# A new issue order for the same instructions: dynamic convolution, LayerNorm and a two-layer FFN on one core

## The chip, the cores and the metric

One NeuronCore of one Trainium2 chip. The metric is device time in microseconds (us), the median of several executions of the whole program.

## What is computed

The inputs are `x` (8 x 4224 x 192, float32), `weight_gen` (8 x 4224 x 8 x 7), a LayerNorm gain and two float64 weight matrices (192 x 768 and 768 x 192). The reference, cut to what matters:

```
w = softmax(weight_gen, axis=-1)                      # 8 heads, 7 taps
y[b,s,h] = sum_k w[b,s,h,k] * x_padded[b, s+k, h]     # causal, 24 channels a head
xn = (y - mean) / sqrt(var + 1e-6) * g_ln
out = y + max(xn @ w_ch1, 0) @ w_ch2
```

## The kernel before

The 33792 tokens lie as 264 columns of 128 partitions. Columns are worked in parts (`PARTS`), parts in chunks of 4 or 6 columns, and the FFN in 66 groups of 4 columns (`NT`).

**Convolution.** For each chunk VectorE (DVE) makes seven products, as three pair instructions and one single one (`mul`, L511). GpSimd (POOL) sums them: two accumulating DMAs (L517, steps `d0`, `d1`) add one half of a pair to the other in memory, and four tensor additions (L514, steps `a0` to `a3`) collect the rest. For the first three chunks (`DIRECT`) TensorE (PE) sums the products with matmuls against an identity (L532, `z0` to `z3`). The softmax weights come in 23 blocks (`SOFT`), spread over DVE, POOL and ScalarE (ACT).

**Norm and transposition.** ACT takes sums and squares of y (L564, L569), scales (`xh`, L615) and rounds to float16 (`hi`, L635); POOL makes the rounding rest (`lo`, L648); a transposing DMA from the SP queue (`turn`, L652) writes `xT`.

**FFN.** A group is three units (`unit`, L670, 36 pairs of matmuls of 64 rows each) and two output halves (`p0`, `p1`, L721, 72 pairs of 64 rows). A unit fills one of two PSUM buffers `ph`. ACT reads it (`relu`, L685, into `hh`), then DVE (`hlo`, L687), and only then can the next unit with that buffer start. PE runs two units of group g, `p0` of group g-1, the third unit, `p1` of g-1. Between the halves an empty SP instruction (`hop`, L731) passes a semaphore on. DVE adds the output to y (`f`, L773) and SP stores it (`u`, L781). The last group's output is made by `output` (L750).

**Weights.** They are brought from float64 to pairs of float16 at the start: `from_double` (L833 to L849), `w_scale` (L860 to L876, with a PE sum, a root on ACT and a reciprocal on DVE), then for the first layer L902 on ACT, the subtraction L905 on POOL and four copies L909 on SP that swap the halves of `c_w`; for the second layer L935 and L936 on ACT and L938 on POOL (all three have the key `w_s2`). `wake` (L642) is 11 matmuls whose result is not used.

**Order.** Nothing is scheduled by the framework (`manual_schedule`). Every step is recorded by `op` with a number from the table `PLACE` (key, then one number for each use), and `Plan.order` issues the steps in the order of these numbers. The numbers also pick buffers: a step that first uses a buffer takes the one whose last user stands earliest. And an accumulating DMA and a transposing one never run together: each waits for the last one of the other kind that stands ahead of it (`o.behind`):

```
for o in plan.order():
    made[o] = o.fn()
    if o.behind:
        tc.add_manual_dep(made[o].ins, made[o.behind].ins.name, apart, reason="transfers kept apart")
```

Of the kernel before, what the change touches and what calls it, by code (L numbers as in the profile page):

```python
# [31 lines left out]
    'wload': (3, 9, 33, 42, 82, 86, 121, 257, 191, 373, 568, 527, 770, 1053, 851, 1068, 1156, 1216, 1427, 1301,  # L32
        1465, 1705, 1809),
    'load': (26, 12, 32, 37, 85, 87, 102, 103, 84, 120, 298, 261, 337, 260, 421, 466, 456, 526, 338, 569, 642,
        641, 756, 712, 769, 783, 849, 885, 978, 1067, 979, 1162, 1159, 1163, 1302, 1343, 1368, 1369, 1572, 1426,
        1566, 1569, 1613, 1806, 1768, 1769, 1808, 1938, 1905, 2076, 2134, 2035),
    'w_load': (40, 11, 13, 0, 1, 2),
    'w_load2': (58,),
    'w_as': (67,),
    'w_av': (41, 44, 65, 73),  # L40
    'w_an': (80,),
    'w_cs': (20,),
    'w_cv': (15, 17, 22, 23),
    'w_cn': (45,),
    'w_s1': (81, 88, 97, 104, 112),
    'w_h': (122, 123, 125, 127),
    'w_l': (153, 156),
    'w_m': (190, 193, 195, 192),
    'w_c2s': (71, 124, 146),
    'w_c2v': (72, 74, 76, 78, 91, 105, 130, 135, 137, 139, 161, 163),  # L50
    'w_c2n': (93, 144, 168),
    'w_s2': (169, 171, 182, 184, 212, 206, 207, 213),
    'max': (4, 10, 34, 43, 89, 136, 138, 352, 234, 446, 665, 608, 868, 1070, 935, 1103, 1258, 1261, 1474, 1430,
        1592, 1712, 1837),
    'sub': (5, 18, 51, 110, 111, 203, 320, 431, 551, 653, 750, 844, 967, 1148, 1090, 1243, 1406, 1441, 1581,
        1684, 1812, 1850, 1947),
    'exp': (6, 19, 52, 115, 114, 227, 321, 436, 552, 659, 751, 860, 983, 1166, 1114, 1255, 1418, 1459, 1582,
        1700, 1825, 1875, 1964),
    'sum': (7, 21, 66, 131, 133, 242, 350, 495, 553, 664, 752, 929, 1009, 1168, 1126, 1260, 1431, 1480, 1591,
        1719, 1834, 1907, 1991),  # L60
    'rcp': (8, 25, 70, 141, 175, 293, 384, 505, 573, 689, 802, 930, 1011, 1170, 1197, 1289, 1501, 1500, 1628,
        1720, 1880, 1960, 2043),
    'inv': (14, 29, 77, 162, 221, 324, 471, 545, 655, 746, 879, 947, 1078, 1202, 1259, 1388, 1536, 1540, 1644,
        1754, 1928, 2006, 2044),
    'mul': (16, 31, 90, 185, 315, 416, 525, 639, 742, 831, 933, 1018, 1128, 1231, 1328, 1433, 1537, 1636, 1738,
        1823, 1930, 2039, 2131),
    'keep': (24, 54),
# [16 lines left out]
    'copy': (53, 94, 126),  # L84
    'sums': (55, 57, 96, 99, 142, 140, 176, 177, 244, 246, 247, 255, 291, 295, 332, 326, 367, 396, 401, 397,
# [7 lines left out]
    'squares': (56, 68, 98, 100, 148, 147, 178, 180, 245, 251, 252, 256, 296, 306, 334, 333, 386, 398, 409, 412,  # L93
# [7 lines left out]
    'rstd': (69, 101, 149, 181, 253, 281, 335, 413, 492, 560, 627, 710, 801, 904, 1001, 1113, 1213, 1298, 1386,  # L101
        1502, 1601, 1702, 1819, 1900, 2005, 2100, 2199, 2285, 2325),
    'newton': (75, 108, 165, 186, 274, 286, 353, 414, 496, 577, 635, 721, 806, 916, 1012, 1116, 1220, 1307,
# [13 lines left out]
    'wake': (208,),  # L117
# [885 lines left out]
```

## Time and profile before

| what | value |
|---|---|
| runs | 869.25 us median (866.22, 869.25, 870.33) |
| profiled execution | span 867.2 us, mean granted TensorE clock 0.987; the page gives no other time for it |
| busy: PE, DVE, ACT, POOL | 95%, 89%, 79%, 78% of the span |
| instructions | 37431 |

The span runs from the first to the last instruction of one execution, and lies inside the spread of the three runs. Times in the rows below are us from the start of that span unless a column says ns. "PEld" is the weight load that runs beside a matmul; "SPq" is a DMA's issue on the SP queue. [...]

### The profile page before, as it was taken

The numbers are of one execution on the slowest core, as the hardware profiler recorded it, in microseconds if no ns is written. First come the engines' busy times: TensorE is split into PE (matmuls) and PEld (weight loads), VectorE is DVE, ScalarE is ACT, GpSimd is POOL, SyncE is SP. The second block draws the span as 40 slices with busy tenths as digits, with TensorE's granted clock in tenths as the row PEclk, the third lists the DMA queues.
The fourth block names the chain that finished last, engine by engine and source line by source line (L and its number), as shares of the span: only waits on it lengthen the run. The fifth ranks groups of instructions, "written<-read, shape, count | busy, mean of one in ns | idle before, by whom it ended". The sixth has DMA issues, their size and how long they took to land.

```text
span 867.2 us, 37431 instructions
## 1 busy us (share of the span) xinstructions
PE 823.4 (95%) x16665; PEld 787.7 (91%) x16665; DVE 772.1 (89%) x796; ACT 683.7 (79%) x1781; POOL 679.6 (78%) x390
## 2 busy tenths in 40 slices
PE   3857999999999999999999999999999999999997
PEld 2526999999999999999999999999989999999997
DVE  6899999999999999999999999999989989874442
ACT  2798898799678889889888789787887888796631
POOL 3399999899889999897887889888976788885100
PEclk9968999999999999999999999999999999999999
DMA  7768868988897958988899698878948569565123
GB/s 193 190 127 166 166 163 184 200 176 180 194 193 151 220 94 188 213 181 180 160 205 195 149 213 175 165 139 187 207 99 200 120 151 190 124 127 106 40 76 110
DMA packets 137465, 140.89 MB, mean 162 GB/s; under 512 B 107479, under 2 KB 109015, under 8 KB 137303
## 3 DMA queue, kind: packets, MB, share of 16 engines
q1 hardware_dynamic: 123175, 88.95, 44.9%
q0 software_dynamic: 13824, 49.55, 29.6%
q8 instruction: 130, 2.13, 1.1%
q14 instruction: 32, 0.26, 0.1%
q10 hardware_dynamic: 304, 0.00, 0.0%
HBM read 36.43 MB, written 25.95 MB: 72 GB/s over the span
## 4 chain that ended last, share of the span: by engine, by line
PE 68%; DVE 9%; issue 2%; DVEq 0%
PE ph L670 34%; PE po L721 34%; DVE pr L511 4%; DVE hlo L687 2%; DVE y L511 1%; DVE y L773 1%; PE ph L750 1%; DVE sm L449 0%; DVE mx L440 0%; DVE wn L465 0%; DVE wn L460 0%; DVE wn L461 0%; DVE wn L459 0%; DVE wn L599 0%; DVE wn L601 0%
## 5 line engine op out<-in xcount | busy, mean ns | idle before, releaser
L514 POOL TENSOR_TENSOR y<-y,pr 128x1152 f32<-128x1152 f32 (+1 forms) x192 | 474.5, 2499 | 39.0 <-DVE pr L511 22.1
L670 PE MATMUL ph<-xT,c_w 64*128 64x256 f16 x7128 | 420.0, 270 | 10.5 <-DVE hlo L687 7.8
L670 PEld LDWEIGHTS <-c_w 64*128 64x128 f16 x7128 | 377.6, 94 | 28.3 <-issue 13.5
L721 PE MATMUL po<-c_w2h,hh 64*128 64x192 f16 x3120 | 392.5, 243 | 1.4 <-issue 1.0
L721 PE MATMUL po<-c_w2h,hlo 64*128 64x192 f16 x3120 | 392.4, 243 | 0.5 <-issue 0.5
L721 PE MATMUL po<-c_w2l,hh 64*128 64x192 f16 x3120 | 392.4, 243 | 0.0
L721 PEld LDWEIGHTS <-hh 64*128 64x128 f16 x6240 | 345.7, 94 | 2.8 <-issue 1.9
L511 DVE TENSOR_TENSOR pr<-x,wn 128x2304 f32<-128x2304 f32 (+1 forms) x150 | 332.5, 2226 | 6.6 <-POOL y L514 1.8
L687 DVE SCALAR_TENSOR_TENSOR hlo<-ph,hh 128x1024 f16<-128x1024 f32 x198 | 239.2, 1219 | 57.2 <-ACT hh L685 56.9
L685 ACT ACTIVATE hh<-ph 128x1024 f16<-128x1024 f32 x198 | 200.3, 1015 | 105.2 <-PE ph L670 101.7
L721 PEld LDWEIGHTS <-hlo 64*128 64x128 f16 x3120 | 225.5, 94 | 0.7 <-issue 0.7
L648 POOL TENSOR_TENSOR hl<-xh,hl 128x768 f16<-128x768 f32 x66 | 115.0, 1748 | 44.5 <-ACT hl L635 33.0
L615 ACT ACTIVATE xh<-y,s 128x192 f32<-128x192 f32 x264 | 125.5, 535 | 16.1 <-DVE s L603 12.5
L569 ACT ACTIVATE junk<-y,s 128x192 f32<-128x192 f32 x264 | 119.6, 453 | 6.9
L517 POOL DMA_DIRECT2D pr<-pr x96 | 94.4, 1082 | 37.3 <-DMA xT<-hl 14.2
L564 ACT ACTIVATE junk<-y 128x192 f32<-128x192 f32 x264 | 95.1, 360 | 13.6 <-POOL y L514 7.2
L773 DVE SCALAR_TENSOR_TENSOR y<-po,c_fs,y 128x768 f32<-128x768 f32 (+1 forms) x80 | 67.9, 860 | 5.4 <-PE po L721 5.4
L511 DVE TENSOR_TENSOR y<-x,wn 128x1152 f32<-128x1152 f32 (+1 forms) x51 | 60.0, 1181 | 0.1
L635 ACT ACTIVATE hl<-xh 128x768 f16<-128x768 f32 x66 | 55.0, 837 | 2.1 <-DMA xT<-hl 1.1
L564 ACT ACTIVATION_READ_ACCUMULATOR junk<-y 128x1 f32 x264 | 49.5, 188 | 0.0
L569 ACT ACTIVATION_READ_ACCUMULATOR junk<-y,s 128x1 f32 x264 | 49.4, 187 | 0.0
L532 PE MATMUL ph<-pr,ident 128*128 128x384 f32 x72 | 27.1, 531 | 16.5 <-DVE pr L511 15.6
(76 smaller groups left out, 298.5 us busy)
## 6 DMA issues: line engine op xcount, KB each, us to landing
pr<-pr POOLq DMA_DIRECT2D x60, 576.0 KB, 7.8
x<-in_x_dram SPq DMA_DIRECT2D x30, 576.0 KB, 6.3
out_dram<-y SPq DMA_DIRECT2D x30, 576.0 KB, 5.2
pr<-pr POOLq DMA_DIRECT2D x36, 384.0 KB, 5.8
x<-in_x_dram SPq DMA_DIRECT2D x20, 384.0 KB, 5.5
out_dram<-y SPq DMA_DIRECT2D x20, 384.0 KB, 5.3
w<-in_weight_gen_dram SPq DMA_DIRECT2D x21, 336.0 KB, 5.8
pr<-in_moe_w_ch_dram SPq DMA_DIRECT2D x1, 1152.0 KB
```

What stands on the lines that cost most here:

```text
L511: E.tensor_tensor(out=ov, in0=xv, in1=wv, op=ALU.mult)
L514: Q.tensor_tensor(out=flat(0), in0=flat(0), in1=flat(k), op=ALU.add)
L517: return Q.dma_start(flat(to), flat(k), accum_op=ALU.add, max_dma_last_dim=CHUNK * D * 4)
L564: A.activation(junk, at(y)[:, j, :], AF.Identity, scale=-1.0 / D, accum_out=at(s4)[:, 3, t : t + 1])
L569: A.activation(junk, at(y)[:, j, :], AF.Square, bias=at(s4)[:, 3, t : t + 1], accum_out=at(s4)[:, 0, t : t + 1])
L615: A.activation(paired(xh, t), at(y)[:, i, :].rearrange("p (c q) -> p c q", q=P // 2), AF.Identity, bias=at(s4)[:, 3, g + t : g + t + 1], s ...
L648: lambda xh=xh, hl=hl: Q.tensor_tensor(out=halves(hl, True), in0=pairs(xh), in1=halves(hl, False), op=ALU.subtract),
L670: T_.matmul(ph[:, r, v * 2 * P : (v + 1) * 2 * P], W["w1"][rows, WB[r][c], w, f : f + P], xv[rows, a, c, :, :], start=(v == 0 and k == 0), ...
L685: lambda: A.activation(at(hh)[:, us, :], at(ph), AF.Relu), [ph], [(hh, u)])
L687: lambda: V.scalar_tensor_tensor(out=at(hlo)[:, us, :], in0=at(ph), scalar=0.0, in1=at(hh)[:, us, :], op0=ALU.max, op1=ALU.subtract),
L721: made.append(T_.matmul(at(po)[:, z, e * D : (e + 1) * D], token(b, 2 * z + e, j)[rows], W[w][rows, j, :], start=(ph == 0 and e == 0 and k ...
L773: V.scalar_tensor_tensor(out=ysl, in0=at(po)[:, zs[0] : zs[-1] + 1, : 2 * D], scalar=W["fs"][:, 0:1], in1=ysl, op0=ALU.mult, op1=ALU.add)
```

## The change

Only the numbers of `PLACE` differ. No step is added or removed, no buffer pool, size or instruction changes; which buffer of a pool a step gets does follow from the new numbers. The table is four lines longer, so every line number behind it grows by 4 (L670 is L674, and so on). PE's order is the same but for one exchange; of DVE's 626 steps 451 stand elsewhere, of ACT's 770 621, of POOL's 383 271, of SP's 266 196, by at most 33 places. The table's rows tell nothing by themselves; the two lines on PE's exchange and the copies of `c_w`:

```diff
-    'wake': (208,),
+    'wake': (159,),
-    'w_s2': (169, 171, 182, 184, 212, 206, 207, 213),
+    'w_s2': (178, 202, 203, 207, 230, 220, 226, 231),
-    'w_m': (190, 193, 195, 192),
+    'w_m': (141, 139, 148, 186),
...
```

On PE, `wake` (11 pairs of L642) now stands ahead of the sum L860 of the second layer's weights; before it stood behind it.

The SP queue just ahead of the first unit (`c_w` is the first layer's weights, `xT` the transposed input, `w` softmax input, `x` the convolution's input). Before:

```order
L909 DMA c_w1_127<-c_w1_127 64x1536
L422 DMA w1_65<-in_weight_gen_dram 128x1x672
L909 DMA c_w1_127<-c_w1_127 64x2x384
L909 DMA c_w1_127<-c_w1_127 64x1536
L652 DMA_TRANSPOSE xT0_85<-hl0_83 128x12x128
L909 DMA c_w1_127<-c_w1_127 64x2x384
L652 DMA_TRANSPOSE xT1_86<-hl1_84 128x12x128
L422 DMA w2_66<-in_weight_gen_dram 128x1x672
```

and now:

```order
L656 DMA_TRANSPOSE xT0_85<-hl0_83 128x12x128
L426 DMA w1_65<-in_weight_gen_dram 128x1x672
L913 DMA c_w1_127<-c_w1_127 64x1536 x2
L913 DMA c_w1_127<-c_w1_127 64x2x384
L420 DMA x_63<-in_x_dram 128x1x768
L656 DMA_TRANSPOSE xT1_86<-hl1_84 128x12x128
L913 DMA c_w1_127<-c_w1_127 64x2x384
```

The first transposition moved ahead of all four copies, and the last copy behind the second transposition. That last copy is also another one: before it filled the upper rows (needed by the second unit), now the lower rows (needed by the first unit's sixth weight load).

POOL in the same stretch (`pr` products, `y` their sum, L648 is `lo`). Before:

```order
L517 DMA pr3_79<-pr3_79 128x768
L648 TENSOR_TENSOR hl0_83<-xh0_81,hl0_83 128x2x384
L514 TENSOR_TENSOR y3_70<-y3_70,pr0_76 128x768
L905 TENSOR_TENSOR c_w1_127<-hlo0_90,c_w1_127 128x768
L517 DMA pr4_80<-pr4_80 128x768
L514 TENSOR_TENSOR y3_70<-y3_70,pr0_76 128x768
L905 TENSOR_TENSOR c_w1_127<-hlo0_90,c_w1_127 128x384
```

and now:

```order
L521 DMA pr4_80<-pr4_80 128x768
L652 TENSOR_TENSOR hl0_83<-xh0_81,hl0_83 128x2x384
L518 TENSOR_TENSOR y3_70<-y3_70,pr0_76 128x768
L909 TENSOR_TENSOR c_w1_127<-hlo0_90,c_w1_127 128x768
L518 TENSOR_TENSOR y3_70<-y3_70,pr0_76 128x768
L909 TENSOR_TENSOR c_w1_127<-hlo0_90,c_w1_127 128x384
L521 DMA pr2_78<-pr2_78 128x768
```

The second accumulating DMA now comes behind the second weight subtraction. In `PLACE` the first transposition follows the first accumulating DMA and the second transposition the second one; before, both followed the second.

ACT around the first two evictions (`hh0<-ph` is `relu` of a unit, L935/L936 the second layer's weights, `c_r2` their root). Before:

```order
L635 ACTIVATE hl1_84<-xh0_81 128x2x384
L935 ACTIVATE hlo1_91<-hlo1_91,c_r2_125 128x1152
L936 ACTIVATE c_w2h_128<-hlo1_91 128x1152
L685 ACTIVATE hh0_88<-ph1_106 128x1024
L928 ACTIVATE c_fs_126<-c_r1_124 128x1
L929 ACTIVATE c_fs_126<-c_fs_126,c_r2_125 128x1
L615 ACTIVATE xh1_82<-y3_70,s40_100 128x3x64 x2
L685 ACTIVATE hh0_88<-ph0_105 128x1024
```

and now:

```order
L689 ACTIVATE hh0_88<-ph1_106 128x1024
L689 ACTIVATE hh0_88<-ph0_105 128x1024
L871 ACTIVATE c_r2_125<-c_r2_125 128x1
L872 ACTIVATE c_r2_125<-c_r2_125 128x1
L456 ACTIVATE rr0_94<-sm0_96,bias_117 128x96
L457 ACTIVATE rr0_94<-rr0_94 128x96
L449 ACTIVATE e1_99<-e1_99 128x672
L619 ACTIVATE xh1_82<-y3_70,s40_100 128x3x64 x4
L639 ACTIVATE hl1_84<-xh1_82 128x2x384
L939 ACTIVATE hlo1_91<-hlo1_91,c_r2_125 128x1152
L940 ACTIVATE c_w2h_128<-hlo1_91 128x1152
```

Both evictions moved ahead of the second layer's weights, and the root L871/L872 behind them. On DVE the reciprocal that uses this root (three steps of `c_r`) now stands directly ahead of the first `hlo`; before it stood ten rows earlier.

## Rows read from the trace of the kernel before

**Rows 1.** The page's first two parts: busy time of an engine with its share of the span, and the granted clock in 40 slices, in tenths.

```profile
PE 823.4 (95%) x16665; PEld 787.7 (91%) x16665; DVE 772.1 (89%) x796; ACT 683.7 (79%) x1781; POOL 679.6 (78%) x390
...
PEclk9968999999999999999999999999999999999999
```

**Rows 2.** The chain of waits in order of time, near its end: start us, us, what.

```profile
806.50 2.97 PE po L721 x72
809.47 3.93 PE ph L670 x72
813.40 2.97 PE po L721 x72
816.37 1.96 PE ph L670 x36
```

**Rows 3.** Stretches of 100 us: length, then busy us and instructions of PE, PEld, DVE, ACT, POOL, then granted clock, DMA share, GB/s.

```profile
300.00:400.00 100.00, 99.98 (x2129) 99.53 (x2125) 99.10 (x92) 86.95 (x230) 91.30 (x48) 1.00 0.85 175
700.00:800.00 100.00, 100.00 (x2133) 99.49 (x2129) 78.60 (x78) 78.62 (x205) 81.10 (x45) 1.00 0.68 137
```

**Rows 4.** Whom PE waited for from 82 us to the end: us in total, times, longest.

```profile
PE ph L670 <- issue: 2.5, 2, 1.4
PE ph L670 <- DVE hlo L687: 2.3, 5, 1.0
PE po L721 <- issue: 1.5, 2, 1.0
```

**Rows 5.** Timeline of PE: the four places where it stood still with "issue" named as the cause (in brackets the idle time before the row).

```profile
420.65 0.25 PE L721 MATMUL po<-c_w2h,hh 64*128 64x192 f16 x1 [1.01 <-issue]
463.85 3.66 PE L670 MATMUL ph<-xT,c_w 64*128 64x256 f16 x63 [1.13 <-issue]
634.46 0.61 PE L670 MATMUL ph<-xT,c_w 64*128 64x256 f16 x7 [1.39 <-issue]
671.24 0.25 PE L721 MATMUL po<-c_w2h,hlo 64*128 64x192 f16 x1 [0.51 <-issue]
```

**Rows 6.** DMA queues from 408.5 to 418.4 us, 9.9 us just ahead of the first of these places: packets, MB, share of 16 engines.

```profile
q0 software_dynamic: 270, 1.13, 64.5%
q1 hardware_dynamic: 216, 0.74, 27.8%
q14 instruction: 2, 0.02, 0.4%
```

**Rows 7.** The same view from 395 to 405 us, 10 us without such a place.

```profile
q0 software_dynamic: 288, 1.18, 59.2%
q1 hardware_dynamic: 119, 0.47, 21.5%
q8 instruction: 2, 0.03, 1.4%
```

**Rows 8.** Groups of DVE instructions by shape: busy us, mean ns | idle before.

```profile
L511 DVE TENSOR_TENSOR y<-x,wn 128x768 f32<-128x768 f32 x21 | 19.6, 946 | 0.0
```

**Rows 9.** Whom DVE waited for from 80 to 400 us.

```profile
DVE pr L511 <- POOL y L514: 0.2, 1, 0.2
```

**Rows 10.** Timeline of all engines around the first unit: start us, us, engine, line, operation.

```profile
50.69 0.87 POOL L517 DMA_DIRECT2D pr<-pr  x1
51.30 2.11 POOL L514 TENSOR_TENSOR y<-y,pr 128x768 f32<-128x768 f32 x1
53.09 1.19 POOL L905 TENSOR_TENSOR c_w<-hlo,c_w 128x384 f16<-128x384 f32 x1
56.39 1.60 SPq L652 DMA_TRANSPOSE xT<-hl  x1
58.05 0.64 SPq L909 DMA_DIRECT2D c_w<-c_w  x1
59.45 4.66 PE L642 MATMUL ph<-hl 128*128 128x512 f16 x11
64.04 4.10 PE L670 MATMUL ph<-xT,c_w 64*128 64x256 f16 x72
66.10 0.20 ACT L868 ACTIVATE c_r<-c_r 128x1 f32<-128x1 f32 x1
67.78 0.16 DVE L876 RECIPROCAL c_r<-c_r 128x1 f32<-128x1 f32 x1
70.33 1.01 ACT L685 ACTIVATE hh<-ph 128x1024 f16<-128x1024 f32 x1
72.08 1.22 DVE L687 SCALAR_TENSOR_TENSOR hlo<-ph,hh 128x1024 f16<-128x1024 f32 x1
73.35 6.08 PE L670 MATMUL ph<-xT,c_w 64*128 64x256 f16 x72 [5.21 <-DVE hlo L687]
81.71 0.26 PE L721 MATMUL po<-c_w2h,hh 64*128 64x192 f16 x2
```

**Rows 11.** DMAs issued from 49 to 64 us: engine, operation, count, KB each, median us from issue to landing.

```profile
pr<-pr POOLq DMA_DIRECT2D x1, 384.0 KB, 5.7
...
c_w<-c_w SPq DMA_DIRECT2D x2, 96.0 KB, 3.9
```

**Rows 12.** Stretches around the first unit, columns as in rows 3.

```profile
64.00:68.00 4.00, 4.00 (x73) 3.52 (x73) 3.93 (x8) 3.18 (x11) 4.00 (x5) 1.00 0.51 98
...
73.00:77.00 4.00, 3.65 (x36) 2.90 (x37) 3.78 (x6) 2.25 (x4) 4.00 (x3) 0.50 0.72 166
```

More of the change, by code (lines that the diff above doesn't have):

```diff
@@ L31 @@
 PLACE = {
[L32 to L47, printed above, removed]
-    'w_m': (190, 193, 195, 192),
-    'w_c2s': (71, 124, 146),
-    'w_c2v': (72, 74, 76, 78, 91, 105, 130, 135, 137, 139, 161, 163),
-    'w_c2n': (93, 144, 168),
-    'w_s2': (169, 171, 182, 184, 212, 206, 207, 213),
-    'max': (4, 10, 34, 43, 89, 136, 138, 352, 234, 446, 665, 608, 868, 1070, 935, 1103, 1258, 1261, 1474, 1430,
-        1592, 1712, 1837),
@@ L55 @@
[L55 to L67, printed above, removed]
[16 rows of a table removed]
-    'copy': (53, 94, 126),
-    'sums': (55, 57, 96, 99, 142, 140, 176, 177, 244, 246, 247, 255, 291, 295, 332, 326, 367, 396, 401, 397,
[7 rows of a table removed]
-    'squares': (56, 68, 98, 100, 148, 147, 178, 180, 245, 251, 252, 256, 296, 306, 334, 333, 386, 398, 409, 412,
[7 rows of a table removed]
@@ L101 @@
-    'rstd': (69, 101, 149, 181, 253, 281, 335, 413, 492, 560, 627, 710, 801, 904, 1001, 1113, 1213, 1298, 1386,
-        1502, 1601, 1702, 1819, 1900, 2005, 2100, 2199, 2285, 2325),
-    'newton': (75, 108, 165, 186, 274, 286, 353, 414, 496, 577, 635, 721, 806, 916, 1012, 1116, 1220, 1307,
[13 rows of a table removed]
-    'wake': (208,),
[4 rows of a table removed]
-    'turn': (194, 196, 258, 259, 336, 375, 418, 417, 462, 463, 565, 564, 646, 648, 702, 701, 782, 785, 848, 883,
[21 rows of a table removed]
-    'halo': (239, 645, 863, 1135, 1370, 1669, 2014),
-    'unit': (209, 210, 224, 228, 232, 249, 264, 279, 288, 302, 304, 328, 341, 342, 369, 379, 388, 406, 423, 426,
[10 rows of a table removed]
@@ L156 @@
-    'relu': (211, 216, 225, 233, 240, 250, 277, 282, 292, 303, 305, 329, 343, 359, 370, 387, 399, 410, 435, 437,
[10 rows of a table removed]
-    'hlo': (220, 222, 226, 236, 241, 254, 283, 284, 297, 317, 319, 331, 354, 360, 380, 389, 400, 411, 442, 445,
[14 rows of a table removed]
-    'hop': (262, 300, 339, 377, 419, 457, 487, 528, 567, 602, 647, 684, 714, 747, 784, 810, 850, 886, 924, 956,
[16 rows of a table removed]
+    'wload': (0, 4, 16, 13, 55, 58, 132, 233, 117, 399, 614, 573, 704, 1024, 850, 1080, 1216, 1195, 1437,
+        1287, 1516, 1708, 1864),
+    'load': (12, 11, 35, 19, 60, 82, 115, 81, 102, 169, 253, 291, 223, 189, 390, 311, 431, 393, 335, 586,
+        641, 564, 748, 665, 796, 788, 858, 829, 993, 1087, 948, 1168, 1115, 1184, 1283, 1355, 1352, 1374,
+        1571, 1417, 1621, 1554, 1567, 1767, 1783, 1751, 1846, 1941, 1991, 2131, 2105, 2034),
@@ new lines @@
+    'w_load': (40, 9, 7, 22, 10, 3),
+    'w_load2': (47,),
+    'w_as': (70,),
+    'w_av': (64, 65, 67, 71),
+    'w_an': (79,),
+    'w_cs': (28,),
+    'w_cv': (23, 29, 30, 41),
+    'w_cn': (42,),
+    'w_s1': (93, 94, 95, 106, 109),
+    'w_h': (112, 114, 127, 134),
+    'w_l': (133, 140),
+    'w_m': (141, 139, 148, 186),
+    'w_c2s': (83, 120, 144),
+    'w_c2v': (66, 68, 73, 84, 98, 122, 126, 138, 145, 146, 147, 158),
+    'w_c2n': (92, 164, 162),
+    'w_s2': (178, 202, 203, 207, 230, 220, 226, 231),
@@ new lines @@
+    'max': (1, 5, 37, 36, 90, 166, 160, 343, 250, 479, 693, 601, 932, 1074, 907, 1107, 1259, 1257, 1475,
+        1500, 1606, 1709, 1912),
+    'sub': (2, 17, 39, 96, 118, 205, 336, 428, 551, 668, 750, 874, 951, 1149, 1060, 1254, 1383, 1428, 1579,
+        1647, 1777, 1875, 1951),
+    'exp': (6, 18, 44, 116, 174, 211, 351, 453, 589, 675, 774, 916, 1004, 1150, 1089, 1267, 1422, 1468,
+        1580, 1667, 1788, 1924, 1968),
+    'sum': (8, 20, 48, 136, 182, 213, 387, 468, 590, 694, 795, 934, 1017, 1165, 1122, 1268, 1448, 1488,
+        1591, 1755, 1844, 1982, 1979),
@@ new lines @@
+    'rcp': (14, 21, 78, 173, 204, 341, 429, 481, 608, 728, 812, 941, 1032, 1183, 1166, 1293, 1497, 1489,
+        1648, 1819, 1885, 2011, 2007),
+    'inv': (15, 27, 80, 187, 212, 345, 510, 538, 688, 761, 851, 1009, 1094, 1208, 1255, 1354, 1530, 1543,
+        1650, 1829, 1896, 2030, 2044),
+    'mul': (24, 34, 97, 190, 308, 423, 537, 650, 747, 834, 929, 1031, 1125, 1224, 1321, 1424, 1531, 1630,
+        1732, 1830, 1926, 2032, 2139),
+    'keep': (25, 50),
[16 rows of a table added]
+    'copy': (53, 87, 124),
+    'sums': (56, 54, 91, 104, 153, 128, 177, 184, 245, 256, 288, 249, 300, 333, 337, 328, 368, 414, 400,
[7 rows of a table added]
@@ new lines @@
+    'squares': (72, 74, 108, 105, 155, 151, 179, 193, 246, 257, 296, 254, 305, 348, 352, 330, 406, 418, 426,
[7 rows of a table added]
+    'rstd': (75, 110, 163, 199, 258, 299, 353, 427, 491, 563, 638, 730, 808, 906, 1013, 1111, 1217, 1303,
+        1405, 1517, 1603, 1716, 1823, 1917, 2014, 2111, 2207, 2286, 2340),
+    'newton': (76, 125, 168, 206, 278, 309, 356, 435, 501, 567, 647, 739, 811, 908, 1014, 1113, 1220, 1310,
[13 rows of a table added]
+    'wake': (159,),
[4 rows of a table added]
+    'turn': (130, 171, 239, 224, 312, 364, 401, 412, 472, 467, 550, 533, 628, 626, 674, 691, 760, 753, 822,
[21 rows of a table added]
@@ L199 @@
+    'halo': (281, 620, 863, 1121, 1367, 1763, 2048),
+    'unit': (191, 196, 227, 236, 237, 248, 266, 269, 292, 302, 303, 324, 339, 355, 358, 388, 395, 404, 409,
[11 rows of a table added]
+    'relu': (200, 201, 228, 238, 243, 251, 267, 271, 293, 314, 317, 326, 349, 360, 362, 389, 397, 417, 434,
[11 rows of a table added]
+    'hlo': (208, 221, 229, 242, 244, 264, 283, 286, 301, 315, 329, 334, 350, 361, 375, 392, 398, 419, 447,
[15 rows of a table added]
+    'hop': (252, 294, 320, 359, 407, 446, 484, 517, 569, 604, 642, 662, 703, 734, 768, 810, 841, 872, 915,
[17 rows of a table added]
 }
```

240 rows, old and new, of the table PLACE are left out of this document.

## The prediction

> **What bounds the kernel now.** I read the page's first two parts first: PE is busy 95% of the span, DVE 89%, and the granted clock is low in the first slices only [rows 1]. So the kernel has a start in which PE has little to do, and then a long stretch in which PE itself is the limit. The chain of waits near the end gives the price of one group there: two units 3.93 us, one half of the output 2.97, one unit 1.96, the other half 2.97, together 11.83 us [rows 2]. At the first output half, at 81.71 [rows 10], five units are done. What is left is 193 units of 1.965 us (379), 130 halves of 2.97 (386), and the last group's output, about 6 us as two such halves (an estimate): 771 us. 81.7 + 771 is 853; the span ends at 867.2. No issue order changes the 771. What an order can change is the start and those 14 us.
>
> For the 14 us I read whom PE waited for from 82 us on: "issue" 4.0 us, and DVE's `hlo` 2.3 us in five waits [rows 4]. The rest is the last output's way to memory and pauses too short to be named.
>
> The DVE waits: in 300 to 400 us DVE is busy 99.10 of 100 us, in 700 to 800 us only 78.60, with PE at 100 in both [rows 3], and from 80 to 400 us DVE itself waited 0.2 us in all [rows 9]. So for the first half of the run DVE is as full as PE, and each microsecond it loses early shows later as a wait for `hlo`.
>
> The "issue" stalls: four gaps of 0.51 to 1.39 us at places where nothing the profile shows was awaited [rows 5]. The DMA queues just ahead of the first one: in 9.9 us the accumulating and other transfers take 64.5% + 27.8% of the DMA engines, and q8 has no packet [rows 6]. In 10 us without such a stall q8 brought two blocks beside 59.2% + 21.5% [rows 7]. I read q8 as PE's instruction fetch, and the gaps as PE having run dry because its blocks came late behind bulk transfers.
>
> **The start, step by step.** Before, `wake` runs from 59.45 for 4.66 us and holds the first unit until 64.04; the copy of `c_w` issued at 58.05 with 3.9 us to landing was there at about 62 [rows 10, 11]. Units 0 and 1 end at 68.14. PE then stands 5.21 us until the first `hlo`, and the next 72 pairs take 6.08 us in place of 3.93 at granted clock 0.50 [rows 2, 10, 12].
>
> Now `wake` runs earlier and holds nothing. What holds the first unit is a chain of transfers:
> - The second accumulating DMA stands behind both weight subtractions. Late end: it is issued where the second one ends now, 53.09 + 1.19 = 54.3 [rows 10]. Early end: its own 0.87 no longer stands ahead, nor, if the products are ready sooner, an addition of 2.11: 51.3 [rows 10].
> - It lands 5.7 us on [rows 11]: 57.0 to 60.0. The second transposition must wait for it; its issue is 1.60 [rows 10]: 58.6 to 61.6.
> - The last `c_w` copy is queued behind that issue on SP, 3.9 us to landing [rows 11]: 62.5 to 65.5. The first five pairs of unit 0 don't need it; the sixth does.
> - The other 67 of 72 pairs come after a pause, so I price them at the slow level, 67/72 of 6.08 = 5.7 us: units 0 and 1 end at 68.2 to 71.2, against 68.14.
> - Then `relu` 1.01, root 2 x 0.20, three reciprocal steps of 0.16, `hlo` 1.22 [rows 10], and 0.3 for hand-overs (an estimate; `hlo` to PE was 0.05): 3.4 us in place of 5.21. DVE is ready: ahead of its first `hlo` the order lists seven single products where it had nine, 1.9 us less [rows 8]. The second layer's weights, which stood between on ACT, now follow the evictions.
>
> The third unit starts at 71.6 to 74.6, against 73.35: -1.8 to +1.3. I take **0**; the shorter pause and the later end of the first units pay for each other. Its slow clock stays in my sum.
>
> **The DVE-bound stretch: 0.** Its loss is set by how much DVE work stands ahead of an `hlo`. At the 54th, 60th and 97th unit both orders list the same DVE work ahead, up to one reduction, under the 0.95 us of a single product [rows 8]. So the 2.3 us of waits [rows 4] may move, but I bound the change by -0.95 and +0.95 and take the middle. Nothing covers it: DVE is as full as PE there [rows 3].
>
> **The instruction fetches: -3.0.** Between one output half and the next I counted, in the order of all steps, the bulk transfers (loads, stores, accumulating DMAs). Stretches with none fall from 53 to 31, those with four or more from 21 to 9, with five or more from 8 to 1. POOL's runs of three or more accumulating DMAs in a row fall from 7 to 3. So the transfers are spread more evenly, and a PE fetch meets fewer pile-ups. No row shows what spreading them is worth. Bounds: 0 (the stalls stay, or new ones come) and -4.0 (all go) [rows 4]. By the share of crowded stretches that vanish it is 4.0 x 12/21 = 2.3 to 4.0 x 7/8 = 3.5; I take 3.0.
>
> The row shows a stall with q8 empty for 9.9 us [rows 6]. The Trainium skill, "Runtime: NRT & Kernel Launch", section "Instruction fetch mechanics", says that the sequencer streams blocks of instructions by its own queue and that the cost of a block boundary is mostly hidden. By it the stalls would not be fetches at all and this term would be 0. The trace speaks against it in four places [rows 5], so I keep the term; what it would make of the time is the third case below.
>
> **The end: 0.** The last group's output stands as before, and DVE and ACT have slack there.
>
> **Sum.** 0 + 0 - 3.0 + 0. The profiled execution has 867.2, so 864.2 in its own terms. The runs' median stands 2.05 above that span; against it the sum is 869.25 - 3.0 = about **866**.
>
> **Rivals.**
> 1. *The start gains too.* All four fetch stalls go (-4.0), the chain of transfers takes its early end (-1.8), and the pause is short enough that the next 72 pairs run at 3.93 rather than 6.08 (-2.15) [rows 2, 10]: 869.25 - 7.95 = 861.3. For it: 3.4 us of pause in place of 5.21. Against it: in the order now, PE also has a pause ahead of the first unit.
> 2. *Nothing is gained.* The late fetches have another cause than crowding between halves, or the stalls only move: 869. For it: the crowded stretches that I counted don't sit exactly at the four places, and SP's runs of three or more bulk transfers go from 20 to 22. This is also the time by the skill's rule.
> 3. *Slower: the last weight copy comes late.* The accumulating DMA of 384 KB now follows two copies and an input load on the same DMA engines. If it and they go one behind the other, it lands 3.9 us later [rows 11], so the copy lands at 69.4, the first two units end at 75.1, and the third unit starts at 78.5, which is 5.1 after 73.35. DVE waits with its reciprocal and the first `hlo`, and since it has 0.2 us of waits in the 320 us that follow [rows 9], what it loses comes out at the end: 869.25 + 5.1 = 874.4 without the fetch gain, 871.4 with it. It decides from a landing at about 65 us; before that the shorter 3.4 us hand-over pays for it. For it: the copy needed first is now issued last. Against it: before, that DMA ran beside two such copies too, and the 5.7 us hold this already.
>
> **How the numbers follow.** My forecast has 0.55, rival 1 0.17, rival 2 0.13, rival 3 without the fetch gain 0.15. The forecast's own range runs from 869.25 - 4.0 - 1.8 = 863.4 to 869.25 - 2.3 + 1.3 = 868.3. About 0.5% (4.35 us) is what a measurement of this kernel can tell from no change: faster means below 864.9, slower above 873.6. Below 864.9 lie rival 1 and some 0.20 of the forecast: 0.37. Above 873.6 lie rival 3 and 0.02 of a worse late start: 0.17. The rest, 0.46, is between. The range leaves out rival 3's upper part and a little of rival 1: 860.5 to 872.0.
>
> **What would show it right or wrong.** In the changed profile: `wake` over before about 59 us; first unit held by SP's copy of `c_w`, third unit starting between 71.6 and 74.6; ACT's two first `relu` ahead of the second layer's weights; a sum of "issue" waits of PE after 82 us near 1 in place of 4.0; `hlo` waits near 2.3. The forecast is wrong if the "issue" waits are as large as before (rival 2), if the third unit starts before 71 with its 72 pairs in about 4 us (rival 1), or if it starts after 76 with DVE idle ahead of it (rival 3). It is wrong in a way I have not priced if DVE shows waits for POOL's additions or for input loads between 80 and 400 us: that stretch has nothing to cover them.

## The result and the profile of the changed kernel

The new order is slower: 876.75 us median of five executions against 868.95, ratio 1.0086 with the interval 1.006 to 1.0112. (One of the five took 4920 us with every matmul several times as long; it is left out of the ratio, and the profile below is of another execution of the same kernel, 878.17 us, span 876.4, the longest of its five usual ones.) The forecast was 866, at least 860.5 and at most 872.

The page's first two parts, as in [rows 1]:

```profile
PE 825.2 (94%) x16665; PEld 794.2 (91%) x16665; DVE 774.7 (88%) x796; ACT 684.8 (78%) x1781; POOL 679.0 (77%) x390
...
PEclk9979999999999999999999999999999999999999
```

The work of every engine is what it was, and so is the granted clock. What grew is idle time of PE. Whom PE waited for from 82 us on, to be set beside [rows 4]:

```profile
PE po L725 <- issue: 4.3, 3, 1.9
PE po L725 <- SPq L735: 3.6, 3, 1.7
PE ph L674 <- issue: 2.6, 2, 1.3
PE ph L674 <- DVE hlo L691: 2.5, 3, 1.6
PE po L725 <- DVE y L777: 1.5, 1, 1.5
PE ph L674 <- DMA xT<-hl: 0.6, 1, 0.6
```

Three things are to be seen. "issue" is 6.9 us where it was 4.0. A wait for SP's `hop` (L735), 3.6 us in three waits, was not in the list before at all. The `hlo` waits are 2.5 after 2.3, but a wait of 1.5 for `f` (the DVE step that frees `po`) replaces one of 0.3. The named waits sum to 15.1 us; before they were 6.6. The difference, 8.5, is nearly the 9.2 us between the two spans.

The stretches of 100 us, as in [rows 3], show when it happens:

```profile
300.00:400.00 100.00, 97.52 (x2066) 93.05 (x2064) 96.68 (x91) 83.78 (x218) 88.44 (x47) 1.00 0.84 168
700.00:800.00 100.00, 100.00 (x2123) 99.79 (x2120) 82.80 (x82) 78.61 (x198) 78.79 (x44) 1.00 0.65 131
```

In 300 to 400 us PE is busy 2.5 us less than before and DVE 2.4, where both had had nothing to spare. Late in the run PE loses nothing in either. Set against the same matmul of the execution before, the new one stands 0.4 us early at 82 us, 0.4 late at 122, 6.2 at 361, 8.2 at 448, 9.9 from 501 to 640, then between 7.6 and 9.3, and 9.2 at the end.

**The start** came out inside the forecast in this execution. Rows of PE, ACT and DVE around the first unit (start us, us), which answer to [rows 10]:

```profile
59.98 0.82 PE L674 MATMUL ph<-xT,c_w 64*128 64x256 f16 x5
62.09 5.91 PE L674 MATMUL ph<-xT,c_w 64*128 64x256 f16 x67 [1.29 <-DMA c_w<-c_w]
72.83 3.81 PE L674 MATMUL ph<-xT,c_w 64*128 64x256 f16 x36 [4.84 <-DVE hlo L691]
...
68.67 1.92 ACT L689 ACTIVATE hh<-ph 128x1024 f16<-128x1024 f32 x2
70.47 0.20 ACT L871 ACTIVATE c_r<-c_r 128x1 f32<-128x1 f32 x1
...
71.50 0.16 DVE L880 RECIPROCAL c_r<-c_r 128x1 f32<-128x1 f32 x1
71.58 1.21 DVE L691 SCALAR_TENSOR_TENSOR hlo<-ph,hh 128x1024 f16<-128x1024 f32 x1
```

Five matmuls run, the sixth waits 1.29 us for the last copy of `c_w`, 67 take 5.91 us with it, and the third unit starts at 72.83, inside the 71.6 to 74.6 of the forecast. (A unit is 36 matmuls and an output half 72: 198 units make the 7128 records of L674. What stands ahead of the result calls each of them a pair.)

This execution was late here. Four kernels of the experiments below (`start_new`, `half_new`, `old_1104_1333`, `old_270_531`) issue the same first 270 steps; in their profiles the third unit starts at 71.33, 71.20, 70.39 and 70.59 us, 2.0 to 3.0 us ahead of the kernel before. The first of them:

```profile
71.33 3.63 PE L670 MATMUL ph<-xT,c_w 64*128 64x256 f16 x36 [5.58 <-DVE hlo L687]
```

**The "issue" waits are late instruction blocks.** The four rows of PE behind 300 us:

```profile
353.00 0.24 PE L725 MATMUL po<-c_w2h,hh 64*128 64x192 f16 x1 [1.91 <-issue]
478.42 0.24 PE L725 MATMUL po<-c_w2h,hlo 64*128 64x192 f16 x1 [1.02 <-issue]
497.88 0.50 PE L674 MATMUL ph<-xT,c_w 64*128 64x256 f16 x6 [1.29 <-issue]
692.40 0.24 PE L725 MATMUL po<-c_w2l,hh 64*128 64x192 f16 x1 [1.33 <-issue]
```

Numbering PE's matmuls from the start of the program gives 5854, 8414, 8798 and 12894 for these, 734 for the fifth at 103.92 us, and 7390, 8286, 11870 and 12638 for the four of [rows 5]. Every one of the nine leaves 94 when divided by 128. A matmul and its weight load are two instructions, so all stand at a boundary of blocks of 256. PE's 16665 matmuls and as many weight loads fill 130 such blocks, and q8 moved 130 packets, 16.4 KB each (2.13 MB): one packet a block. The DMA queues in the 9.9 us ahead of the stall at 353:

```profile
q0 software_dynamic: 197, 0.76, 44.1%
q1 hardware_dynamic: 288, 0.93, 32.7%
q8 instruction: 1, 0.02, 0.6%
```

One block in 9.9 us, where [rows 7] had two in 10. The times of the packets themselves settle it. The same view for 343 to 350.6 us, and then for 350.6 to 352.9:

```profile
q0 software_dynamic: 194, 0.76, 57.4%
q1 hardware_dynamic: 262, 0.88, 40.3%
```

```profile
q1 hardware_dynamic: 26, 0.06, 7.6%
q8 instruction: 1, 0.02, 2.6%
```

Bulk transfers held 97.7% of the DMA engines, and only behind them the block began to move, at 350.68 us, 6.1 us after PE had reached the block before it. It landed at 351.62, and PE went on at 353.00. So it is at all five stalls: the packet begins 4.7 to 6.1 us after PE has reached the block before, and PE goes on 1.3 to 1.6 us after it has landed. At the other 123 boundaries behind 82 us the packet begins at most 3.9 us after (median of all 128: 1.0). In the kernel before it is 4.2 to 5.4 us at the four stalls and at most 3.8 elsewhere (median 0.8); [rows 6] end at 418.4, and the packet that PE then waits for begins at 418.43.

**The waits for `hop`.** The chain of waits between 410 and 444 us, whole pieces over 0.4 us:

```profile
410.55 8.75 DMA xT<-hl
...
420.17 8.12 DMA pr<-pr
...
428.42 3.29 DMA xT<-hl
...
432.25 0.44 POOL pr L521
...
434.47 1.94 POOL hl L652
436.40 5.17 POOL y L518 x2
441.57 0.69 SPq L656
...
442.31 0.60 SPq L420
...
442.96 0.59 SPq L426
...
443.67 2.40 PE po L725 x53
```

PE does not stand in this chain for 33 us. (It was working meanwhile, and waited for `hop` twice, 1.28 us at 430 and 1.71 us at 444.) A transposing DMA lands, releases two accumulating ones (issued at 419.59), and their landing releases the next transposition at 428.42; that releases the next accumulating DMA, then come POOL's rests `lo` and two additions, then two more transpositions and, behind them on SP's queue, a load of `x`, one of `w`, and the empty `hop` that `p1` needs. Before, the chain in the same part of the program held PE alone:

```profile
410.70 2.97 PE po L721 x72
413.67 3.93 PE ph L670 x72
417.60 2.04 PE po L721 x49
419.64 1.01 issue
420.65 1.16 PE po L721 x23
```

SP waited 20.2 us for accumulating DMAs from 414 to 444 us, and 11.2 us from 406 to 440 in the kernel before. The rule that keeps the two kinds of transfers apart makes this loop, and the new order closes it more often: going through all 162 of them in order, the kind changes 75 times where it changed 63 times, and from an accumulating DMA to the transposition that must wait for it there are 15 places at the median where there were 28. The count is no price: run 5 below has 73 changes and no such wait in the stretch that it puts back. No run took the rule itself away, so what it costs is read from this chain and not measured alone.

### The profile page after: what moved, and what is told of

It reads as the page before. It is cut to its first block, busy times and chain, and to the rows that moved or that the text cites. A ratio compares the mean times of both kernels' runs of the same rounds, so it can differ in the third digit from the quotient of the medians.

```text
span 4918.5 us, 37452 instructions
## 1 busy us (share of the span) xinstructions
PE 4897.1 (100%) x16665; PEld 2751.1 (56%) x16665; DVE 792.8 (16%) x796; ACT 694.5 (14%) x1781; POOL 676.7 (14%) x390
## 2 busy tenths in 40 slices
DMA packets 137465, 140.89 MB, mean 29 GB/s; under 512 B 107479, under 2 KB 109015, under 8 KB 137303
## 3 DMA queue, kind: packets, MB, share of 16 engines
q8 instruction: 130, 2.13, 0.2%
## 4 chain that ended last, share of the span: by engine, by line
PE 100%; DMA 0%; DVE 0%; SPq 0%; ACT 0%; issue 0%; DVEq 0%
PE ph L674 48%; PE po L725 47%; PE ph L536 3%; PE ph L754 1%; PE ph L646 0%; DMA x<-in_x_dram 0%; PE po L864 0%; DVE pr L515 0%; SPq L426 0%; SPq L807 0%; DVE hlo L691 0%; ACT hh L689 0%; DVE y L777 0%; SPq L413 0%; ACT c_r L872 0%
## 5 line engine op out<-in xcount | busy, mean ns | idle before, releaser
L674 PE MATMUL ph<-xT,c_w 64*128 64x256 f16 x7128 | 2404.1, 1043 | 3.1 <-DVE hlo L691 3.1
L674 PEld LDWEIGHTS <-c_w 64*128 64x128 f16 x7128 | 1140.8, 320 | 1173.5 <-issue 1173.4
L725 PE MATMUL po<-c_w2h,hlo 64*128 64x192 f16 x3120 | 1370.5, 878 | 0.0
L725 PE MATMUL po<-c_w2h,hh 64*128 64x192 f16 x3120 | 1370.3, 878 | 0.0
L725 PE MATMUL po<-c_w2l,hh 64*128 64x192 f16 x3120 | 1370.1, 878 | 0.0
L725 PEld LDWEIGHTS <-hh 64*128 64x128 f16 x6240 | 999.7, 320 | 589.5 <-issue 583.0
L725 PEld LDWEIGHTS <-hlo 64*128 64x128 f16 x3120 | 500.1, 321 | 273.0 <-issue 273.0
L536 PE MATMUL ph<-pr,ident 128*128 128x384 f32 x72 | 144.7, 2373 | 13.9 <-DVE pr L515 13.9
L536 PEld LDWEIGHTS ph<-pr,ident 128*128 128x128 f32 x72 | 65.8, 921 | 85.3 <-issue 85.2
L446 POOL TENSOR_TENSOR e<-w,mx 128x672 f32<-128x672 f32 (+2 forms) x23 | 30.0, 1305 | 153.5 <-DVE wn L469 138.8
```

Of the source, the lines that this page charges most:

```text
L536: T_.matmul(at(z)[:, b, :h], ident, flat(k)[:, b * h : (b + 1) * h], start=(first and k == ks[0]), stop=(last and k == ks[-1]))
L674: T_.matmul(ph[:, r, v * 2 * P : (v + 1) * 2 * P], W["w1"][rows, WB[r][c], w, f : f + P], xv[rows, a, c, :, :], start=(v == 0 and k == 0), ...
L725: made.append(T_.matmul(at(po)[:, z, e * D : (e + 1) * D], token(b, 2 * z + e, j)[rows], W[w][rows, j, :], start=(ph == 0 and e == 0 and k ...
```

## The experiments

Ratios are to the kernel before, run on the same chip; its median was between 868.0 and 869.0 us each time, so medians can be set side by side. Where a kernel takes its numbers of `PLACE` partly from the one order and partly from the other, the diff shows two lines of them.

**1. The changed kernel again**, for the profile above. No edit.

> The changed kernel once more, for a profile with PE at its usual clock. Its runs so far have a median of 876.75 us against 868.95. If the loss is at the start (the last weight copy late), the third unit starts at 78 to 81 us in place of 73.35 and the waits of PE after 82 us stay near 6 us. If it is in the stretch in which DVE is full, the third unit starts at 71 to 75 us and PE's waits for hlo grow from 2.3 to about 10 us. If it is instruction fetches, PE's issue waits grow from 4 to about 11 us.

878.17 us. The third unit starts at 72.83, and both "issue" and `hop` grew, but none of the three as far as its theory asked: the third unit not at 78 to 81, `hlo` at 2.5 and not 10, "issue" at 6.9 and not 11. None of the three theories named the `hop`.

**2. Which part of the program?** The new order up to a place, then the old one, and the reverse.

```diff
 start_new, against before:
-    'wake': (208,),
+    'wake': (159,),
 half_new: also
-    'hop': (262, ..., 1269, 1303, ...
+    'hop': (252, ..., 1250, 1292, ...
```

> The first 270 steps of the new order (to just behind the first output half p1), then all other steps in the old order. Theory start: the whole loss is here, about 876.5 us, ratio 1.008 to 1.009 to the kernel before. Theory DVE stretch and theory fetches: 867 to 870, ratio 0.998 to 1.002.

866.23 us, ratio 0.998 (0.9968 to 0.9991).

> The first 270 steps of the old order, then all other steps in the new order. Theory start: 866 to 869 us (866 if spreading the transfers is still worth 3 us). Theory DVE stretch and theory fetches: 875 to 877.

879.25 us, ratio 1.0124 (1.0096 to 1.0151).

> The first 1304 steps of the new order (the first 55% of all), then the old order. Theory start and theory DVE stretch: 875 to 877 us. Theory fetches: if the new stalls are spread over the run, about half of the loss, 872 to 874.

873.1 us, ratio 1.0056 (1.0038 to 1.0074). So the new start is worth 2.1 us, as its early third unit says, and the theory "start" falls. (The first two medians lie 0.8 and 2.3 us outside what the other theories expected: none had the start gain.) The steps from 270 to 1304 cost about 6.9 us (873.1 against 866.2), the rest of the run some 3 to 4 more.

**3. Which engines?** A mix by engine behind step 270.

```diff
 sppool_old, against the changed kernel:
-    'turn': (..., 1246, 1281, 1277, ...
+    'turn': (..., 1265, 1281, 1273, ...
```

> First 270 steps new; behind them SP and POOL issue their steps in the old order, PE, DVE and ACT in the new one (46 of ACT's and DVE's steps shift a little to allow it). Theory apart (the new order alternates accumulating and transposing DMAs more often, 75 switches against 63, so transpositions go out late and hold the hop behind them on SP): nearly the whole loss behind step 270 is gone, 866 to 869 us, and PE's waits for SP and for xT, 5.8 us in the new order, fall under 1. Theory DVE/ACT: the loss comes from VectorE's and ScalarE's new order, 875 to 877.

915.11 us, ratio 1.0534 (1.0504 to 1.0563).

> The complement: first 270 steps new; behind them DVE and ACT in the old order, SP, POOL and PE in the new one. Theory apart: 873 to 877 us, with PE's waits for SP and xT at 3 to 6 us. Theory DVE/ACT: 866 to 869.

924.35 us, ratio 1.0649 (1.0634 to 1.0665).

> First 270 steps new; behind them only the accumulating and the transposing DMAs take their old places (65 switches), all other steps of POOL, SP, DVE, ACT and PE the new ones. Theory apart: PE's waits for SP and xT go (-5 to -6 us), 869 to 872 us; the instruction fetches keep their 5 to 7 us. Rival (the load of the DMA engines as a whole, not the order of these two kinds): no change from 876.5.

1020.4 us, ratio 1.1757 (1.173 to 1.1784). All three missed every expectation, and they decide nothing between the theories: a mix brings waits of its own. In the last one PE waited for transpositions 63.6 us and POOL for its accumulating DMAs 110.4:

```profile
PE ph L669 <- DMA xT<-hl: 63.6, 15, 10.2
...
POOL y L513 <- DMA pr<-pr: 110.4, 25, 10.6
```

They do show how long PE and POOL can wait for these two kinds of DMA when the steps around them were ordered for other places.

**4. Less traffic.** The output stores cut to one column of four or six, in the new and in the old order.

```diff
-                        tokens(out, t0, n), at(y)[:, i : i + n, :].rearrange("p t d -> p (t d)")),
+                        tokens(out, t0, 1), at(y)[:, i : i + 1, :].rearrange("p t d -> p (t d)")),
```

> The new order with each output store cut to the first column of its chunk (1 of 4 or 6): the rest of the output is left out. 26 MB of stores become about 5 MB; the SP issues stay. If PE's issue waits are instruction fetches that come late behind bulk transfers, they fall from 6.9 us to 3 or less, and the time to 871 to 874. If they have another cause, they stay at 5 to 7 us and the time at 875 to 878. The waits for SP and xT stay in both.

868.01 us, ratio 1.0008 (0.9988 to 1.0028).

> The kernel before with the same cut of the output stores (one column of each chunk is stored, the rest of the output is left out). Control for the run of the new order with cut stores, 868.0. If the new order's loss is that its waits meet the stores' traffic, the old order gains much less than the new one's 8.5 us: 865 to 868, and the gap between the two orders shrinks from 8 to 3 us or less. If less traffic helps every order alike, the old order gains as much: 859 to 862, and the gap stays at 7 to 9 us.

866.35 us, ratio 0.9982 (0.9971 to 0.9992). The new order gains 8.7 us against its 876.75, the old one 1.6: of the gap of 7.8 us 1.7 is left (2.3 by the ratios). PE's waits in the new order with cut stores:

```profile
PE ph L674 <- DVE hlo L691: 3.4, 5, 1.6
PE ph L674 <- issue: 2.4, 1, 2.4
PE po L725 <- DVE y L777: 1.8, 2, 1.5
PE po L725 <- issue: 0.5, 1, 0.5
```

"issue" fell from 6.9 to 2.9, as the theory of late blocks had it (the time fell further than its 871 to 874), and the waits for `hop` and `xT` are gone, which I had not expected: the accumulating DMAs of 576 KB, untouched, land in 6.4 us at the median where they took 7.5. The waits for DVE did not fall (5.2 after 4.0).

**5. The old order in one stretch**, that of the two long `hop` waits.

```diff
-    'turn': (..., 1246, 1281, 1277, ...
+    'turn': (..., 1268, 1280, 1271, ...
-    'hop': (..., 1250, 1292, ...
+    'hop': (..., 1269, 1303, ...
```

> The new order, with the steps from 1104 to 1333 (about 372 to 450 us) issued in the old order. Theory apart: the two long waits for the hop in that stretch (1.28 and 1.71 us at 430 and 444 us, behind transpositions that went out late) go; the time at the end of the stretch stands 2 to 3 us better and stays so, 873 to 875. Rival (DVE sets the pace there and takes the gain back): no change, 876 to 877.

872.97 us, ratio 1.0051 (1.003 to 1.0071): 3.8 us less than the changed kernel, a little more than the 3.0 us of the two waits, though the twelve executions spread from 868.0 to 876.0. In that stretch PE waits for nothing but one block:

```profile
PE po L720 <- issue: 0.7, 1, 0.7
```

**6. Shifting the blocks.** 64 tiny matmuls, where PE was idle, move every block boundary by half a block.

```diff
+                    for k in range(64):
+                        T_.matmul(at(wb)[:, 0, :8], h[:, :P], h[:, :8], start=True, stop=True)
```

> The new order, with 64 tiny unused matmuls behind the wake ones, so that PE's instruction blocks of 128 pairs begin half a block elsewhere in the program. If the issue waits are late instruction blocks, they still stand at the same remainder of the matmul's number by 128, but at other places of the program (none within 1 us of work of the old ones), and their sum changes: 2 to 9 us, time 872 to 880. If they belong to places of the program, they stay at the same steps.

873.13 us, ratio 1.006 (1.0041 to 1.0079). Its waits:

```profile
PE ph L676 <- DVE hlo L693: 2.6, 4, 1.6
PE po L727 <- SPq L737: 2.5, 3, 1.6
PE po L727 <- DVE y L779: 1.9, 2, 1.1
PE po L727 <- issue: 0.8, 3, 0.3
PE ph L676 <- issue: 0.2, 1, 0.2
```

The six that are left (two are under the 0.15 us at which the list begins) again stand at the remainder 94, now at other matmuls of the program; "issue" in the list fell from 6.9 to 1.0. The waits for DVE stayed (4.5 after 4.0), those for `hop` fell to 2.5 and that for `xT` is gone. So the stall belongs to the block and to what the DMA engines carry when it is fetched, not to the step. (This profiled execution has a span of 867.7, below the kernel's median; the 3.6 us of the medians is the size to keep, and with executions from 869.5 to 875.7 it is good to some 2 us.)

> The same 64 tiny matmuls in the kernel with the new start and the old order behind it (866.2). Its issue waits were 2.4 us in the profile. By the theory of late blocks they move and change: 864 to 870 us. The start itself should stay within 1 us, since PE had 3.9 and 3.7 us of idle time there.

868.46 us, ratio 1.0003 (0.999 to 1.0016). The same shift makes a kernel 2.2 us slower (866.23 without it, ratio 0.998) whose block waits were 2.3 us in the profile; they came to 2.1 in an execution of 865.83, the shortest of the twelve, so where the 2.2 us went isn't shown. Which fetches meet a crowd changes with where the blocks begin, and the shift is no remedy.

**7. Shorter accumulating DMAs**, in both orders.

```diff
-            return Q.dma_start(flat(to), flat(k), accum_op=ALU.add, max_dma_last_dim=CHUNK * D * 4)
+            return Q.dma_start(flat(to)[:, :D], flat(k)[:, :D], accum_op=ALU.add, max_dma_last_dim=CHUNK * D * 4)
```

> The new order with each accumulating DMA cut to the first of its 4 or 6 columns (the other columns' sums are left out). Theory apart: transpositions wait for accumulating DMAs, so with shorter ones they go out earlier: PE's waits for SP (3.6 us) and the 1.6 us at the sixth group go, the shortest time from a transposition's issue to its unit rises above 5 us, and with less traffic the block waits fall too: 862 to 867 us. If the transpositions are late for another reason (POOL, ACT), these waits stay: 868 to 873, the fetches' share alone.

864.96 us, ratio 0.996 (0.9948 to 0.9973).

> Control: the order before with the same cut. It has no such waits to lose; only its 4 us of block waits can go: 863 to 867 us. Theory apart: the two orders come within 2 us of each other. Rival: a gap of 4 us or more stays.

866.07 us, ratio 0.9975 (0.9965 to 0.9984). The new order gains 11.8 us, the old one 2.2 to 2.9, and now the new order is the faster one by 1.1. PE's waits in the new order:

```profile
PE ph L674 <- DVE hlo L691: 3.1, 4, 1.6
PE po L725 <- DVE y L777: 1.5, 1, 1.5
PE po L725 <- issue: 0.9, 2, 0.6
```

The `hop` waits are gone and all but two blocks come in time, with the accumulating DMAs landing in 3.3 us. The packets of q8 now begin 0.0 us at the median after PE has reached the block before, in both orders, where it was 1.0 and 0.8. Two details of the expectation failed. The wait of 1.6 us ahead of the sixth group stayed; it is a wait for `hlo`, as the row says, and I had put it down to a late transposition. And the shortest time from a transposition's issue to its unit stayed at 4.5 us, so that number is no sign of lateness.

**8. The old order in the first stretch.**

> The new order with the steps from 270 to 531 (about 85 to 165 us) in the old order. In the new order's profile this stretch loses 2.6 us against the old one (a block wait of 1.27 us at 104, a wait of 1.61 us at 135 ahead of the sixth group). If lost time in a stretch adds up without being taken back, 873 to 875 us; if DVE sets the pace in it anyway, 876 to 877.

The edit is of the kind of 5, on the steps from 270 to 531: `'turn': (..., 337, 375, ...` in place of `312, 364`. 876.73 us, ratio 1.0106 (1.0087 to 1.0124): no gain. The stretch itself lost 1.1 us in the profile in place of 3.1, but a wait of 2.4 us for `f` at 591 us, which the changed kernel didn't have, took that back. Ahead of `f` on DVE stands the maximum of a softmax block (`mx`), and it waited for its input:

```profile
DVE mx L439 <- DMA w<-in_weight_gen_dram: 2.7, 1, 2.7
```

That load went out at 580.05 us and took 9.3 us to land, where loads of its size take 6.2 at the median. Run 5 has the same wait at the same matmul (2.6 us, a landing of 9.5). In the changed kernel the load took 6.8 us and PE came there only at 595.6. So a third kind of transfer that lands late holds back what a repair ahead of it gains.

The fastest kernel with the whole output is that of the new start with the old order behind it, 866.23 us. Its gain is 0.2% (0.1 to 0.3%).

## Why the prediction was wrong

**The fetch term (-3.0) failed, in its sign.** The reading was right: the "issue" waits are instruction blocks that come late behind bulk transfers; the remainder 94, the packets' own times, the shift and the cut stores all bear it out. The step from there failed. I counted how many bulk transfers are issued between two output halves and took fewer crowded stretches for fewer late blocks. A count of issues says neither how long a transfer takes nor what it runs beside. In the new order the blocks cost 6.9 us in place of 4.0, in one execution of each (`start_old`, also with the new order, has 4.9, `start_new`, with the old one, 2.3). The fetches didn't come sooner: of 128 blocks 16 begin over 3 us late where 15 did. I had written the bounds as 0 to -4.0, with "or new ones come" beside the 0 and no price; the upper end had to lie above nothing.

The Trainium skill, "Runtime: NRT & Kernel Launch", section "Instruction fetch mechanics", has the cost of a block boundary as mostly hidden. In the trace that holds for all but five of 130 blocks, and those five cost 6.9 us.

**A wait was left out: `hop`.** It stands in the code, and the prediction put it at nothing without a reason: it speaks of transpositions waiting for accumulating DMAs at the start alone. Of a step that moved I had to ask what is queued behind it on SP in the steady state too: [rows 11] give 5.7 us for the landing that a transposition must wait for, and the distance between the two had halved in the table. That was 3.6 us in the profile; run 5 took the two long waits away, run 7 all of them.

**The start (0) was mis-sized, in the kernel's favour.** That the one profile of the changed kernel has the third unit at 72.83, inside the range, was luck: with the same first steps it starts at 70.4 to 71.3 in four other profiles, and on the chip the start alone gave 2.1 us (0.8 to 2.8 by the interval) where I took 0. Two errors evened out in part. The copy landed at 62.1, and at 59.1 to 60.4 in the four, ahead of the 62.5 to 65.5; why it was so much earlier there isn't shown. The pause was 4.84 us (4.8 to 5.7) and not 3.4, because ACT began its evictions 0.67 us behind the units and did both (1.92 us) before the root.

**The DVE term (0) was right for `hlo`** (2.5 after 2.3), and missed `f`, for which PE waited 1.5 us where it had waited 0.3. Together that is 1.4 us, past the bound of 0.95.

**The rivals.** The first had the start right in part: it gained about what its early end of the transfers gives, 1.8 us. The third, slower, had the sign and the wrong place: the last copy of `c_w` held PE for 1.3 us only. What made the kernel slower lies in the middle of the run: late blocks, and the rule that keeps transfers apart.

What stays open: how the 8 us divide exactly. The profiled executions give +2.9 for blocks, +3.6 for `hop`, +0.2 for `hlo`, +1.2 for `f`, +0.6 for `xT`. The cuts of traffic in 4 and 7 take the first two away together, so they don't tell the rule that keeps transfers apart from the mere load on the DMA engines. Run 5 takes away two of the three `hop` waits and leaves 5.4 us of block waits, run 6 takes away most block waits and a third of the `hop` waits (3.8 and 3.6 us of the medians, each good to some 2 us), but what one stretch gives back can be taken again later, as in 8.

## What to carry to other kernels

Where two kinds of transfers exclude each other, count how often an order changes from one kind to the other and how much work lies between, as a sign of where to look and not as a price; each change can put a landing time in series, and what is queued behind the waiting step on its in-order queue waits too. Before a stall with no named cause is put down to the program, number the instructions at which it comes: a constant remainder points to the instruction fetch, and the times of the fetch's packets show whether it was late. And a mix of two good orders by engine is not an order: test by stretches of time, where few steps straddle the cut, and let a control run tell whether a cut helps both sides.

## What the runs showed of the hardware that was not expected

The landing time of an untouched transfer depends on the rest: accumulating DMAs of 576 KB landed in 7.5 us at the median with full stores and in 6.4 with 20.8 MB of stores less (140.89 to 120.05 MB in all), and transpositions in 4.0 and 3.6 us; in the old order it was 7.8 and 6.8, and 3.7 and 3.5. Instruction blocks queue behind bulk transfers as data does: in the two orders PE stood still at the four and five of 128 boundaries where the block's packet began over 4.1 us after PE had reached the block before, and went on 1.2 to 1.6 us after the landing. And sixty-four matmuls of 8 columns in PE's idle time, which move where its blocks begin, made one kernel 3.6 us faster and another 2.2 us slower.
